# Three of thirty-two zero stores of a decode backward kernel move to GpSimd's queue in pairs of rows, three others to earlier spots on SyncE

## The chip, the cores and the metric

The kernel runs on one core of a Trainium2 chip. The metric is the device time of one execution in microseconds (us). The profile is of one execution of its own; it counts its span from the first instruction of the program to the last.

## What is computed

One decode step of a transformer layer and its gradients, all in bf16, for 4 sequences with one new token each. Cut to what matters:

```python
xn  = layernorm(x)                                     # x: [4, 1, 512]
q   = (xn @ wq)                                        # 32 heads of 128, 8 kv heads
k,v = cache[:, :, Sk - W:, :]                          # Sk = 4096, W = 1024: only the last quarter
out = x + softmax(q k^T / sqrt(128)) v @ wo + (gelu(xn @ w_gate) * (xn @ w_up)) @ w_down
grads = vjp(out)(grad_out)    # of x, k_cache, v_cache, wq, wo, w_gate, w_up, w_down
```

The gradients of the two caches have the caches' whole shape, [4, 8, 4096, 128]. The first 3072 of the 4096 positions take no part in the attention, so their gradients are zero, and the kernel must write those zeros: 2 caches x 4 sequences x 8 heads x 3072 x 128 numbers of two bytes are 50.3 MB. That is 45% of all the bytes that the kernel moves (112.12 MB).

## The kernel before

**Stages.** The feed-forward part comes first (its weights are loaded at the start; its weight gradients are out_6, out_7 and out_8). Then a loop `for t in range(NT)` goes over four groups of two kv heads. Each turn has `pre(t)` (transposed weights, queries and output gradients of the group), `kv_steps(t, 0, ...)` and `kv_steps(t, 1, ...)` (scores with K and with V), the softmax forward and backward, `odq` (the sums over keys), and `fin(t)`. The outer products that make the weight and cache gradients are small pieces in a list `bg`, which `tick(n)` works off between the other steps; each piece evacuates one PSUM bank into a staging tile, and the last piece of a tile stores it.

**The zeros.** `ztile` is a tile of 128 partitions x 6144 zeros. `zlist` holds 32 regions, each two heads of one sequence in out_2 or out_3 (1536 KB). `zero(n)` (L161) takes n regions off the list, or as many as are left, and stores each with one DMA from SyncE (L164) in 128 rows of 12,288 bytes, which all sixteen DMA engines share alike. Calls of `zero` stand at fixed spots of the program: two regions at the start (L168), one after the second `osb_d` store (`zero(f4 == 1)`, L666), one after the first `osb_g` store of each of two weights (L678), one after each store of a cache gradient (L490), two at L721 and in the first turn (L728, L730), `zero(3)` in the last turn (L734), and L755 stores what is left when all else has been issued.

**Queues.** All of SyncE's DMAs go out in program order through one queue. SyncE keeps eight completion semaphores, used in turn, so that a DMA is issued only after the one eight places before it has landed; a store also waits for the engine that fills its tile, and everything behind it waits with it. GpSimd (POOL) issues only the weights of turns 1 to 3, `load_w(t)`, through a queue of its own: `wo_sb` at L123, `wq_sb` at L125. On POOL, `load_w(2)` and `load_w(3)` follow the products `domr` and `qmr` at the end of `pre(1)` and `pre(2)` (L329).

**Buffers.** The pool `stage` holds three staging tiles for the cache gradients (stg_dv, stg_dk), `outp` four for the weight gradients (osb_d, osb_g, osb_o, osb_q). A piece that needs a fresh tile waits until the store of the tile's earlier content has landed. `store` (L100) declares that the stores write disjoint parts of the outputs, so that no store waits for another one for that reason.

Of the kernel before, what the change touches and what calls it, by code (L numbers as in the profile page):

```python
# [18 lines left out]
def kernel(  # L19
# [28 lines left out]
    nc = tc.nc  # L48

    B, Sq, D = A_x.shape  # L50
    _, G, Sk, Dh = A_k_cache.shape
# [4 lines left out]
    K0 = Sk - W  # L56
# [99 lines left out]
    ZR = 2  # L156
    ZW = K0 * Dh * ZR // P
    ztile = const.tile([P, ZW], BF16, name="ztile")
    zlist = deque((og, b, g) for b in range(B) for g in range(0, G, ZR) for og in (out_2, out_3))

    def zero(n=1):  # L161
        for _ in range(min(n, len(zlist))):
            og, b, g = zlist.popleft()
            store(nc.sync, og[b, g:g + ZR, 0:K0, :].rearrange("g (m j) d -> m g (j d)", m=P // ZR), ztile[:], "zeros")  # L164


    nc.gpsimd.memset(ztile[:], 0.0)  # L167
    zero(2)  # L168
    ident_f = const.tile([P, P], FP32, name="ident_f")
    nc.vector.tensor_copy(out=ident_f[:], in_=ident[:])  # L170
    one_f = const.tile([1, 1], FP32, name="one_f")
# [113 lines left out]
    def pre(t):  # L285
        wo_sb, wq_sb = wo_t[t], wq_t[t]
        dq_ps = ps_x.tile([P, 2, HG, B], FP32, name="doq_ps", tag="x")
        held = []

        def do(h2, woT):  # L290
            for i in range(2):
                for c in range(ND):
                    nc.tensor.matmul(dq_ps[:, 0, slot(2 * h2 + i), :], lhsT=woT[:, i, c, :], rhs=dyT[:, c, :],
                                     start=(c == 0), stop=(c == ND - 1))

        for h2 in range(HG // 2):
            ps = transposes([wo_sb[:, 2 * h2 + i, c * P:(c + 1) * P] for i in range(2) for c in range(ND)], "woT")
            woT = tsb.tile([P, 2, ND, P], BF16, name="woT", tag="wT")
            evac(woT[:].rearrange("p i c d -> p (i c d)"), ps[:].rearrange("p x d -> p (x d)"), 1024, half=True)
            held.append((h2, woT))  # L300
            for h in (2 * h2, 2 * h2 + 1):
                for c in range(ND):
                    nc.tensor.matmul(dq_ps[:, 1, slot(h), :], lhsT=wq_sb[:, c, h * Dh:(h + 1) * Dh], rhs=xnT[:, c, :],
                                     start=(c == 0), stop=(c == ND - 1))
            tick(1)
            link()
            if h2:
                do(*held[h2 - 1])
            tick(1)
            link()  # L310
        do(*held[-1])
        T4 = []
        for k, (sc, zt, nm) in enumerate(((None, dom_all[t % 2], "do"), (scale, qm_all[t % 2], "qs"))):
            xT4 = attw.tile([P, B, HG, NQ], BF16, name=nm + "T4", tag=nm + "T4")
            src = dq_ps[:, k].rearrange("p h b -> p b h").unsqueeze(3).broadcast_to([P, B, HG, NQ])
            if sc is None:
                nc.vector.tensor_copy(out=xT4[:], in_=src)
            else:
                nc.scalar.activation(out=xT4[:], in_=src, func=ACT.Copy, scale=sc)
            nc.vector.tensor_copy(out=zt[:, :, SL - 1:].rearrange("p (b g) (r s) -> p b g r s", g=GP, s=SL)[:, :, :, :, 0],  # L320
                                  in_=xT4[:, :, :, 0].rearrange("p b (r g) -> p b g r", g=GP))
            T4.append(xT4)
        tick(2)
        r_ps = transposes([x[:].rearrange("p b h q -> p (b h q)") for x in T4], "r")
        r4 = attw.tile([P, 2, Dh], BF16, name="r4", tag="r4")
        nc.vector.tensor_copy(out=r4[:], in_=r_ps[:])  # L326
        for k, nm in enumerate(("do", "q")):
            mr = attw.tile([P, GP, NQ, Dh], BF16, name=nm + "mr", tag=nm + "mr", bufs=2)
            nc.gpsimd.tensor_tensor(out=mr[:].rearrange("p g q d -> p (g q) d"),  # L329
                                    in0=r4[:, k, :].unsqueeze(1).broadcast_to([P, SL, Dh]),  # L330
                                    in1=msk[:].unsqueeze(2).broadcast_to([P, SL, Dh]),
                                    op=ALU.mult)
            st[t][nm] = mr

    def kv_steps(t, k, links):

# [318 lines left out]
    def piece_d(f4, i, n, held):  # L655
        if i == 0:
            held["osb"] = outp.tile([P, 4, D], BF16, name="osb_d", tag="o")
        m = n * P // 4
        mps = ps_w.tile([P, D], FP32, name="dwd_ps", tag="w")
        nc.tensor.matmul(mps[0:m], lhsT=a_s[:, f4].rearrange("p i f -> p (i f)")[:, i:n * P:4], rhs=dyr[:],  # L660
                         start=True, stop=True)
        evac(held["osb"][0:m, i, :], mps[0:m], 512)
        if i == 3:
            store(nc.sync, out_8[4 * f4 * P:(4 * f4 + n) * P, :].rearrange("(p i) n -> p (i n)", i=4),
                  held["osb"][0:m].rearrange("p i n -> p (i n)"), "rest")
            zero(f4 == 1)  # L666

    def piece_g(s_r, og, c, i, held):
        if i == 0:
# [47 lines left out]
    with tc.tile_pool(name="kv_b", bufs=GP, reuse_waits="tile") as kv_b, \  # L717
            tc.tile_pool(name="w_b", bufs=1, reuse_waits="tile") as w_b, \
            tc.tile_pool(name="stage", bufs=3, reuse_waits="tile") as stage:
        kv_pool[1], w_pool[1] = kv_b, w_b  # L720
        zero()  # L721
        pre(0)
        load_w(1)
        load_kv(1, 0)
        for t in range(NT):
            kv_steps(t, 0, 0)
            if t == 0:
                zero()  # L728
                load_kv(1, 1)
                zero()  # L730
            softmax(t)
            kv_steps(t, 1, 1)
            if t == NT - 1:
                zero(3)  # L734
            link(len(chain))
            softmax_d(t)
            link()
            odq(t, 0)
            load_kv(t + 2, 1)
            if t + 1 < NT:  # L740
                pre(t + 1)
            link(len(chain))
            odT(t, 0)
            odq(t, 1)
            load_kv(t + 2, 0)
            tick(2)
            odT(t, 1)
            fin(t)
            if t + 2 < NT:
                load_w(t + 2)  # L750
            (k0, k1), (o0, o1, q0, q1) = dvdk(t, 1), dw(t)
            for p in (k0, o0, k1, o1, q0, q1):
                bg.extend(p)
        tick(len(bg))
        zero(len(zlist))  # L755

        fin_ps = []
        for o in range(2):
            f_ps = ps_w.tile([B, ND, P], FP32, name="f_ps", tag="w")
            for c in range(ND):  # L760
                nc.tensor.transpose(f_ps[:, c, :], acc[:, o, c, :], ident_f[:])
            fin_ps.append(f_ps)
        acc_o = fin_ps[0][:].rearrange("b c p -> b (c p)")
        acc_d = attw.tile([B, P, ND], FP32, name="acc_d", tag="P_s")
        nc.vector.tensor_copy(out=acc_d[:].rearrange("b p c -> b c p"), in_=fin_ps[1][:])
        acc_d = acc_d[:].rearrange("b p c -> b (p c)")
        out_b = attw.tile([B, D], BF16, name="out_b", tag="pT")
        nc.vector.tensor_tensor(out=out_b[:], in0=acc_o, in1=x4[:], op=ALU.add)
        nc.scalar.dma_start(out=out_0.rearrange("b s d -> (b s) d"), in_=out_b[:])

        s1 = attw.tile([B, 1], FP32, name="s1", tag="m")
        nc.vector.reduce_sum(out=s1[:], in_=acc_d, axis=AX.X)
        pr = attw.tile([B, D], FP32, name="pr", tag="dS_s")
        s2 = attw.tile([B, 1], FP32, name="s2", tag="es")
        nc.vector.tensor_tensor_reduce(out=pr[:], in0=acc_d, in1=xn_f[:], scale=1.0, scalar=0.0,
                                       op0=ALU.mult, op1=ALU.add, accum_out=s2[:])
        nm1 = attw.tile([B, 1], FP32, name="nm1", tag="rr")
        nc.vector.tensor_scalar(out=nm1[:], in0=s1[:], scalar1=-1.0 / D, scalar2=None, op0=ALU.mult)
        nm2 = attw.tile([B, 1], FP32, name="nm2", tag="gs")
        nc.vector.tensor_scalar(out=nm2[:], in0=s2[:], scalar1=-1.0 / D, scalar2=None, op0=ALU.mult)  # L780
        nc.vector.scalar_tensor_tensor(out=pr[:], in0=xn_f[:], scalar=nm2[:, 0:1], in1=acc_d,
                                       op0=ALU.mult, op1=ALU.add)
        nc.vector.tensor_scalar(out=pr[:], in0=pr[:], scalar1=nm1[:, 0:1], scalar2=rstd[:, 0:1],
                                op0=ALU.add, op1=ALU.mult)
        dx_b = attw.tile([B, D], BF16, name="dx_b", tag="E_f")
        nc.vector.tensor_tensor(out=dx_b[:], in0=pr[:], in1=dy4[:], op=ALU.add)
        nc.scalar.dma_start(out=out_1.rearrange("b s d -> (b s) d"), in_=dx_b[:])
# [30 lines left out]
```

## Time and profile before

| what | value |
|---|---|
| median of three runs | 284.95 us (284.80 to 285.53) |
| the profiled execution's own time | 285.34 us |
| its span | 283.4 us |
| busy: PE / DVE / ACT / POOL | 200.5 / 163.4 / 117.8 / 40.1 us |
| moved by DMA | 112.12 MB, mean 396 GB/s |
| SyncE's queue, share of 16 DMA engines' span | 89.5% |
| POOL's queue, the same | 5.6% |
| ACT's queue, the same | 1.8% |
| the 32 zero stores | 1536 KB each, median 19.4 us from issue to landing |

The page of a profile has one part with the span in 40 equal slices of 7.1 us: a digit for each engine (9 is busy for 90% or more), the mean busy share of the sixteen DMA engines, and what they moved. Busy time of the computing engines is an average over the span; here none of them is busy for more than 71% of it, and all of them end well before the span does.

### The profile page before, as it was taken

The page shows a single profiled execution, that of the slowest core. Times are in us where ns is not written, and L with a number is a line of the kernel's source. Part 1 is how long each engine was busy: PE and PEld are TensorE (multiplying, and loading weights), DVE is VectorE, ACT ScalarE, POOL GpSimd, SP SyncE. Part 2 cuts the span into 40 slices and gives each one's busy share as a digit, 9 for nine tenths or more (in the row PEclk, how much of TensorE's full clock was granted, in tenths as well). Part 3 has the DMA queues.
Part 4 walks back from the last instruction along what each step waited for, and adds up shares of the span by engine and source line. Part 5 has one row for each costly group of instructions (what it writes and reads, how often), then busy time and mean ns, then how long its engine had stood idle before and what let it go on. Part 6 is the DMA issues. An engine that isn't in the chain of part 4 may idle for free.

```text
span 283.4 us, 6866 instructions
## 1 busy us (share of the span) xinstructions
PE 200.5 (71%) x2972; PEld 137.3 (48%) x2972; DVE 163.4 (58%) x313; ACT 117.8 (42%) x219; POOL 40.1 (14%) x40
## 2 busy tenths in 40 slices
PE   0275799998798899998993799889995997300000
PEld 0264576765466754676752467665564743100000
DVE  7946646676857455767561576766776288900000
ACT  2021476662156077635371464438661387200000
POOL 8600000043011700020700002130004000000000
PEclk9999579999999999999999599999999799955555
DMA  7999989999999999999999999999999989999993
GB/s 266 391 376 433 432 334 369 370 418 351 366 428 409 419 422 422 426 427 417 410 387 423 423 426 430 410 425 404 397 415 377 415 337 420 426 418 415 422 418 153
DMA packets 19565, 112.12 MB, mean 396 GB/s; under 512 B 1664, under 2 KB 4496, under 8 KB 11088
## 3 DMA queue, kind: packets, MB, share of 16 engines
q1 hardware_dynamic: 17744, 103.56, 89.5%
q0 software_dynamic: 1632, 6.29, 5.6%
q10 hardware_dynamic: 160, 1.84, 1.8%
q8 instruction: 23, 0.38, 0.5%
q14 instruction: 6, 0.05, 0.0%
HBM read 30.68 MB, written 81.01 MB: 394 GB/s over the span
## 4 chain that ended last, share of the span: by engine, by line
PE 30%; issue 19%; DMA 18%; DVE 12%; POOL 5%; ACT 3%; DVEq 0%; POOLq 0%; ACTq 0%
DMA out_dram<-stg_dv 11%; DMA wq_sb<-in_A_wq_dram 7%; PE kv_ps L484 6%; PE T_ps L279 5%; PE od_ps L450 4%; PE S_ps L345 4%; DVE dS_s L367 2%; DVE T_sb L98 2%; PE dwq_ps L520 2%; POOL ztile L167 2%; DVE wqT L98 2%; PE pT_ps L279 2%; PE acc_ps L256 1%; PE dwo_ps L505 1%; DVE P_s L367 1%
## 5 line engine op out<-in xcount | busy, mean ns | idle before, releaser
L98 DVE COPY T_sb<-T_ps 128x1024 bf16<-128x1024 bf16 x64 | 44.1, 688 | 24.9 <-PE T_ps L279 24.7
L97 ACT CAST stg_dk<-kv_ps 128x512 bf16<-128x512 f32 x52 | 29.1, 588 | 26.3 <-PE kv_ps L484 11.5
L97 ACT CAST stg_dv<-kv_ps 128x512 bf16<-128x512 f32 x51 | 28.1, 588 | 25.1 <-PE kv_ps L484 24.4
L484 PE MATMUL kv_ps<-qmr,dS_s 128*128 128x512 bf16 x64 | 23.0, 396 | 7.3 <-ACT stg_dk L97 6.6
L463 POOL TENSOR_TENSOR o_s<-od_r,msk_r 128x512 bf16<-128x512 bf16 x8 | 9.1, 1158 | 107.9 <-DVE od_r L455 78.6
L484 PE MATMUL kv_ps<-domr,P_s 128*128 128x512 bf16 x64 | 21.1, 379 | 0.0
L279 PE MATMUL T_ps<-ident,vb 128*128 128x128 bf16 x256 | 20.3, 225 | 0.3 <-DVE T_sb L98 0.3
L279 PEld LDWEIGHTS <-vb 128*128 128x128 bf16 x256 | 17.2, 101 | 4.9 <-issue 2.7
L279 PE MATMUL T_ps<-ident,kb 128*128 128x128 bf16 x256 | 19.5, 219 | 0.0
L279 PEld LDWEIGHTS <-kb 128*128 128x128 bf16 x256 | 16.7, 98 | 4.2 <-issue 0.9
L97 ACT CAST osb_q<-dwq_ps 128x512 bf16<-128x512 f32 x25 | 14.5, 586 | 8.3 <-PE dwq_ps L520 7.4
L329 POOL TENSOR_TENSOR domr<-r,msk 128x1024 bf16<-128x1024 bf16 x4 | 7.6, 1892 | 68.4 <-DVE r L326 62.0
L97 ACT CAST osb_o<-dwo_ps 128x512 bf16<-128x512 f32 x24 | 13.8, 586 | 4.4 <-PE dwo_ps L505 3.6
L97 ACT CAST osb_g<-dwg_ps 128x512 bf16<-128x512 f32 (+1 forms) x25 | 12.5, 541 | 6.6 <-PE dwg_ps L673 5.0
L98 DVE COPY wgT<-wgT_ps 128x1024 bf16<-128x1024 bf16 x14 | 9.6, 686 | 7.7 <-PE wgT_ps L279 7.7
L345 PE MATMUL S_ps<-T_sb,qm 128*32 128x256 bf16 x128 | 12.7, 386 | 0.6 <-DVE T_sb L98 0.5
L345 PE MATMUL S_ps<-T_sb,dom 128*32 128x256 bf16 x128 | 12.7, 387 | 0.1
L98 DVE COPY woT<-woT_ps 128x1024 bf16<-128x1024 bf16 x16 | 11.0, 686 | 2.6 <-PE woT_ps L279 2.2
L98 DVE CAST stg_dk<-kv_ps 128x512 bf16<-128x512 f32 x12 | 7.9, 686 | 7.8 <-DMA out_dram<-stg_dv 7.2
L505 PE MATMUL dwo_ps<-dyr,o_s 128*128 128x512 bf16 x32 | 11.9, 388 | 0.5 <-DVE stg_dk L98 0.2
L520 PE MATMUL dwq_ps<-od_r,xnm 128*128 128x256 bf16 x64 | 11.6, 274 | 0.2 <-ACT osb_q L97 0.2
L98 DVE COPY wqT<-wqT_ps 128x1024 bf16<-128x1024 bf16 x16 | 10.5, 685 | 1.8 <-PE wqT_ps L279 1.6
(188 smaller groups left out, 377.7 us busy)
## 6 DMA issues: line engine op xcount, KB each, us to landing
out_dram<-ztile SPq DMA_DIRECT2D x32, 1536.0 KB, 19.4
kb<-in_A_k_cache_dram SPq DMA_DIRECT2D x8, 1024.0 KB, 15.7
vb<-in_A_v_cache_dram SPq DMA_DIRECT2D x8, 1024.0 KB, 20.7
out_dram<-stg_dv SPq DMA_DIRECT2D x8, 1024.0 KB, 16.7
out_dram<-stg_dk SPq DMA_DIRECT2D x8, 1024.0 KB, 16.1
out_dram<-osb_o SPq DMA_DIRECT2D x8, 512.0 KB, 19.0
out_dram<-osb_q SPq DMA_DIRECT2D x8, 512.0 KB, 11.6
out_dram<-osb_g SPq DMA_DIRECT2D x8, 448.0 KB, 7.9
```

What stands on the lines that cost most here:

```text
L97: return nc.scalar.copy(out=out, in_=in_)
L98: return nc.vector.tensor_copy(out=out, in_=in_)
L167: nc.gpsimd.memset(ztile[:], 0.0)
L279: nc.tensor.transpose(ps[:, i, :], a, ident[:])
L329: nc.gpsimd.tensor_tensor(out=mr[:].rearrange("p g q d -> p (g q) d"), in0=r4[:, k, :].unsqueeze(1).broadcast_to([P, SL, Dh]), in1=msk[:]. ...
L345: nc.tensor.matmul(ps[b * RB:(b + 1) * RB, :], lhsT=zt[:, b * GP + g, c0:c0 + RB], rhs=T_sb[:].rearrange("p (x b) -> p b x", b=B)[:, b, :] ...
L367: nc.vector.scalar_tensor_tensor(out=out[:], in0=src[:].unsqueeze(2).broadcast_to([P, WQ, B]), scalar=rr[:, 0:1], in1=mskb[:].unsqueeze(1) ...
L450: nc.tensor.matmul(od_ps[g * 32:g * 32 + B * rep, k, g, :], lhsT=cols[:, jj, g * NQ + q, :], rhs=blks[(t, g)][:, j, :], start=(j == 0), st ...
L463: nc.gpsimd.tensor_tensor(out=o_s[:, g], in0=rows[:, g].unsqueeze(1).broadcast_to([P, rep, Dh]), in1=msk_r[:].unsqueeze(2).broadcast_to([P ...
L484: nc.tensor.matmul(mps[:].rearrange("p q d -> p (q d)"), lhsT=src[:, j * P:(j + 1) * P], rhs=mr[:, g].rearrange("p q d -> p (q d)"), start ...
L505: nc.tensor.matmul(mps[:], lhsT=o_s[:, g].rearrange("p r d -> p (r d)")[:, i:rep * Dh:rep], rhs=dyr[:], start=True, stop=True)
L520: nc.tensor.matmul(mps[:, i].rearrange("p g d -> p (g d)"), lhsT=xnm[:, i2 * 2 + i, c * P:(c + 1) * P], rhs=dq_r[:].rearrange("p g d -> p ...
```

## The change

- A new function `zero_pairs()` takes one region off the list and stores it from POOL with eight DMAs of two rows each (one row in each of the region's two heads). Seven of them write 16 x 3456 numbers per row (110,592 bytes); the third (i = 2) writes only the 6144 numbers (12,288 bytes) that are left. The source of DMA i is partition 8i for one row and 8i + 4 for the other; the seven large ones read the same 3456 zeros sixteen times over.
- `zero_pairs()` is called at the end of `pre(t)` for t = 1, 2 and 3. On POOL the eight DMAs stand between `qmr` and `load_w(t + 1)`; those of t = 3 stand before the last two `o_s` products.
- `zero(2)` at the start becomes `zero(3)`; `zero(f4 == 1)` becomes `zero(f4 % 2)`, which also stores one region after the fourth `osb_d` store; `zero(3)` in the last turn becomes `zero(4)`.
- The list of 32 regions is then used up earlier. On SyncE the zero store after the last `stg_dk` and the five at the end are gone; SyncE issues 29 zero stores and POOL the other three regions. Because of the 24 new DMAs on POOL's eight completion semaphores, `load_w(2)` and `load_w(3)` now also wait until the first and second, respectively, of the eight pair stores ahead of them have landed (`wo_sb` for one, `wq_sb` for the other).
- PE, DVE and ACT get the same instructions in the same order.

```diff
+    def zero_pairs():
+
+        if not zlist:
+            return
+        og, b, g = zlist.popleft()
+        zr = og[b, g:g + ZR, 0:K0, :].rearrange("g m d -> g (m d)")
+        w = 27 * Dh
+        r0 = 0
+        for i in range(8):
+            n = 16 * w if i != 2 else K0 * Dh - 7 * 16 * w
+            if i != 2:
+                src = ztile[8 * i:8 * i + 8, 0:w].rearrange("(a x) w -> a x w", a=2)[:, 0, :].unsqueeze(1).broadcast_to([2, 16, w])
+                dst = zr[:, r0:r0 + n].rearrange("g (r w) -> g r w", r=16)
+            else:
+                src = ztile[8 * i:8 * i + 8, 0:n].rearrange("(a x) w -> a x w", a=2)[:, 0, :]
+                dst = zr[:, r0:r0 + n]
+            store(nc.gpsimd, dst, src, "zeros")
+            r0 += n
+
...
     nc.gpsimd.memset(ztile[:], 0.0)
-    zero(2)
+    zero(3)
...
             st[t][nm] = mr
+        if t:
+            zero_pairs()
...
                   held["osb"][0:m].rearrange("p i n -> p (i n)"), "rest")
-            zero(f4 == 1)
+            zero(f4 % 2)
...
             if t == NT - 1:
-                zero(3)
+                zero(4)
```

## The prediction

> **What bounds the kernel now.** I read the page's 40 slices first, then SyncE's DMA issues in order of time, the waits of SyncE, the chain that ended last, and POOL's timeline.
>
> The slices (digits, then GB/s) and the totals:
>
> ```profile
> span 283.4 us, 6866 instructions
> DMA  7999989999999999999999999999999989999993
> GB/s 266 391 376 433 432 334 369 370 418 351 366 428 409 419 422 422 426 427 417 410 387 423 423 426 430 410 425 404 397 415 377 415 337 420 426 418 415 422 418 153
> HBM read 30.68 MB, written 81.01 MB: 394 GB/s over the span
> ```
>
> The DMA engines are the bound: they are busy in nearly every slice, at 415 to 430 GB/s, and slow down in a few places only. The end is pure DMA. Columns of the next two fences: start, length, what, count.
>
> ```profile
> 18.55 1.69 SPq L103 DMA_DIRECT2D out_dram<-ztile  x2
> 37.73 3.53 SPq L103 DMA_DIRECT2D out_dram<-osb_d  x2
> 43.08 3.79 SPq L103 DMA_DIRECT2D out_dram<-osb_d  x2
> 49.16 0.33 SPq L103 DMA_DIRECT2D out_dram<-osb_g  x1
> 211.52 3.15 SPq L103 DMA_DIRECT2D out_dram<-osb_q  x2
> 214.72 3.80 SPq L103 DMA_DIRECT2D out_dram<-ztile  x3
> 228.66 0.54 SPq L103 DMA_DIRECT2D out_dram<-stg_dv  x1
> 253.96 6.89 SPq L103 DMA_DIRECT2D out_dram<-ztile  x5
> ```
>
> The five last zero stores (7.9 MB) are issued when everything else is done. SyncE has nothing to issue around 41, 48 and 228 us, and the queue runs dry there. The waits of SyncE and the chain:
>
> ```profile
> SPq L813 <- DMA out_dram<-ztile: 21.2, 5, 6.7
> ...
> 65.59 18.90 DMA wq_sb<-in_A_wq_dram
> ...
> 132.89 23.57 DMA out_dram<-stg_dv
> ...
> 228.66 7.99 DMA out_dram<-stg_dv
> ...
> 247.74 0.68 DVE dx_b L786
> ```
>
> At the end SyncE waits 21.2 us for five zero stores. Compute ends at 248.4 us, 35 us before the span, so it has slack, and three of its own stalls are on DMAs. POOL:
>
> ```profile
> 94.35 1.89 POOL L329 TENSOR_TENSOR qmr<-r,msk 128x1024 bf16<-128x1024 bf16 x1
> 96.18 0.93 POOL L123 DMA_DIRECT2D wo_sb<-in_A_wo_dram  x1
> 97.73 0.76 POOL L125 DMA_DIRECT2D wq_sb<-in_A_wq_dram  x1 [0.61 <-PE wqT_ps L279]
> ```
>
> Two more readings come from the trace's DMA records. First, each DMA has sixteen completions, one for each engine. Those of the very last store come at 279.0 to 279.2 (fourteen), 279.9 and 282.3 us, so one engine, call it A, sets the end and another, B, is second. A is behind all along: 6.7 us at 156, 6.9 at 190, 5.1 at 221. Followed back from its last packet, A shows no gap of more than 0.06 us down to 71 us: it never idles, so filling the dry spots gives A nothing after 71 us. A's sequence also has no room for the four-row stores of out_0 and out_1, which use four engines. Second, in 2 us bins the mean idle time of an engine is about 1.2 us at 40 to 42, 1.05 at 48 to 52 (together 2.25), and after 196 us 2.5 in five spots, 1.2 of it at 228.
>
> [...]while GpSimd's weights (4,096-byte packets) run beside SyncE's larger ones, at 100 to 116 us, they get 118 to 147 of about 423 GB/s.[...]
>
> **The change part by part.** The bytes stay the same; what can change is idle time, the balance of the engines, and compute's slack.
>
> *Balance.* One region gives each engine 1536 KB / 16 = 98,304 bytes. As pairs it gives fourteen engines 110,592 and two 12,288. Three regions take 258 KB from the two; at 26.2 bytes/ns (a 12,288-byte packet of the before trace takes 0.469 us on average) that is 9.85 us less. The other fourteen get 36.9 KB more, 1.45 us at 25.5 bytes/ns (between the 4,096- and 8,192-byte packets' 24.6 and 25.7). If the two are A and B, A would end at 282.3 - 9.85 = 272.5 and no longer decides. The third engine, D, then does (279.2 us).
>
> *Early fills.* The third store at the start covers the dry spot at 41, the one after the fourth osb_d that at 48 to 51. D idles there about as the mean does, so up to 2.25 us go; I take 2.0. Cost: every osb_d and osb_g store behind them lands up to 3.6 to 7.4 us later (1536 KB at 425 GB/s is 3.7 us), and outp has four tiles, so the feed-forward part may stall for 0 to 3 us. That is compute time, covered by its slack.
>
> *Late fills.* The 2.5 us after 196 belong to the fast engines. D, like A, was behind at each of these spots (2 us at 225) and hardly idled; the fills bring D about 0.2 us at most. I count nothing; at best, if D's lag is shaken up by the new order, 2 us.
>
> [...]I take 0.5 in all, since the weights that ran beside the stores showed no loss of total throughput (423 GB/s).
>
> *POOL's issue and the weights behind it.* Eight issues of 0.76 to 1.06 us each (the wo_sb and wq_sb rows) are 6 to 8.5 us; load_w(2) moves from 96.2 to about 104. It also waits for the first two pair stores, and on each ring its packets stand behind theirs. 110,592 bytes per engine at 40% of 26 bytes/ns are 10.6 us, so the pairs run from 97 to between 108 and 114; wo_sb and wq_sb (128 KB per engine at the 126 GB/s of before) take 16.6 us more: 124 to 130. In before wq_sb landed at 119.7 and was needed at about 126. So pre(2) stalls 0 to 4 us; load_w(3) before landed at 162 and is needed at 174, so it stalls 0 to 1. The pairs of t = 3 have only two o_s products behind them, needed late. Of these DMAs' waits nothing reaches the end of the span unless compute loses its slack.
>
> *Compute's slack.* The last matrix product of the pieces ends at 242.4, dx_b lands at 253.9: 11.5 us later. Before it stand six more regions than in before, 22 us if each delayed it fully; 242.4 + 22.2 + 11.5 = 276, still just under the DMA end below. zero(4) in the last turn lengthens the stg waits at 228 by up to 3.7 us; this is in the 22.
>
> *The last five stores.* They vanish from the end (18.3 us of transfers), but their bytes delay what went before, so as such this gains nothing.
>
> Sum: 279.2 - 2.0 + 1.45 + 0.5 = 279.15 us for D, then 1.1 us from last completion to the span's end (282.3 to 283.4): span 280.2, or 3.2 us less. The profiled execution took 285.34, of which 1.96 lie outside the span, and is 0.39 above the median; against the median: 284.95 - 3.2 = 281.75. Some of the late fill should reach D, because its lag comes and goes; with 0.75 of the 2 us I say 281.0.
>
> **Rivals.**
> - *A is not 4 or 5.* For it: nothing in the profile names A; one engine only is far behind, and it might be any of the twelve that out_0 leaves. Against: the two engines that are behind at the end fit a pair. A then gets 1.45 us more and regains what it idled before 71 us, at most 1: about 285.4, no difference.
> - *Late weights (slower than before).* Place: POOL and its ring at pre(2) and pre(3). If the pair stores get 20% instead of 40% of an engine they last 21 us; wo_sb and wq_sb land some 11 us later still, and the stalls are about 14 and 8 us. With 7 from the early stores and 4 from zero(4), 242.4 + 33 = 275, plus 11.5 is 287, plus 1.1 and 2: about 289. It decides once compute's last product comes after 270, that is from 28 us of delay on. For it: 65.59 18.90 above shows how slow that queue is beside a full one. Against: A's smaller lag frees the stage tiles earlier (in the 23.57 us wait A was the last by 6.7), which gives compute time back.
> - *The pairs don't walk.* If all eight used the same two engines, these would get 786 KB each per region instead of 98, 27 us more, 81 for three: about 360. Slower by far. For it: the profile shows no store of two rows on POOL's queue.[...]
> - *Everything balances.* If all idle time is filled for every engine, 279.0 - 4.75 + 1.45 = 275.7, 6.6 us below 282.3: 278.3.
>
> **How the numbers follow.** Forecast 281.0 (279 to 283.5): 0.48. Full balance 278.3: 0.14. A elsewhere, 285.4: 0.15. Late weights, 289: 0.16. No walk, 360: 0.07. This measurement can tell about 0.3%, 0.85 us, from no change: faster means under 284.1, slower over 285.8. Faster: the first two and some of the third, 0.65; same 0.11, from the third; slower 0.24. The range from 277.0 to 287.5 leaves out the fifth case and the worse part of the fourth; the likeliest case's own range is 279 to 283.5.
>
> **What would show it.** Right: the last store's completions lie within about 2 us, none 3 us behind; no dry spot at 41 and 48; POOL's queue carries 11 MB instead of 6.3; SyncE's last wait is no longer 21 us; dx_b lands before the last store. Wrong: one engine still 3 us behind (A elsewhere); PE waiting over 8 us for wo_sb or wq_sb in pre(2) (late weights); two completions far after all others (no walk). What would make the forecast wrong most easily is D: its 279.2 comes from one profiled execution.

## The result, and the profile after

| kernel | median (range) | runs |
|---|---|---|
| before | 285.12 us (284.80 to 285.53) | 4 |
| after | 323.92 us (321.13 to 326.36) | 4 |

The ratio is 1.133, with a 95% interval from 1.125 to 1.140: the change costs 38.8 us. The forecast was 281.0 us. The profiled execution took 326.36 us, the longest of the four, and the ratio leaves it out (as it does for the run with nine long rows below). Its span is 324.6 us, 41.2 us more than that of before.

The page of the changed kernel, its slices, its DMA totals, its queues (q1 is SyncE's, q0 POOL's, q10 ACT's: packets, MB, share of the 16 engines' span) and the row of the pair stores among its DMA issues (8.1 us per slice here):

```profile
span 324.6 us, 6889 instructions
...
DMA  7999999999999999998209999982099999999992
GB/s 292 373 406 427 429 419 426 421 396 384 425 420 423 422 398 400 374 352 349 116 2 358 380 401 382 362 283 106 0 359 281 320 385 407 422 420 420 425 368 86
DMA packets 24942, 112.15 MB, mean 345 GB/s; under 512 B 6746, under 2 KB 9578, under 8 KB 16842
...
q1 hardware_dynamic: 17312, 98.84, 76.5%
q0 software_dynamic: 7440, 11.03, 10.3%
q10 hardware_dynamic: 160, 1.84, 1.6%
...
out_dram<-ztile POOLq DMA_DIRECT2D x21, 216.0 KB, 31.0
```

Three things are to be seen. The dry spots at 41 and 48 us of before are gone (slices 6 to 8 now carry 419, 426 and 421 GB/s). In their place the DMA engines stand idle twice, in slices 20 and 21 and in 28 and 29 (down to 2 and 0 GB/s); by the DMA records an engine idles on average 15.2 us between 130 and 175 us and 15.7 between 200 and 250. And while the bytes are the same to 0.03 MB, there are 5,377 more packets, 5,082 of them under 512 bytes, although no row of the new stores is shorter than 6,912.

Idle time isn't all of the loss. The shares of the three queues come to 88.4% of 324.6 us here and to 96.9% of 283.4 us before, 287 and 275 us of packet time per engine. So some 29 of the 41.2 us are more idle time of the engines, and 12 are more time in packets.

Why the engines stand idle is in the waits (engine and line, what it waited for: us in total, times, longest) and in the chain that ended last (start, length):

```profile
ACT stg_dv L97 <- PE kv_ps L505: 79.4, 20, 32.6
...
PEld L298 <- DMA wo_sb<-in_A_wo_dram: 44.4, 2, 24.4
PE woT_ps L298 <- DMA wo_sb<-in_A_wo_dram: 44.1, 2, 24.3
...
POOL wo_sb L123 <- PE kv_ps L505: 22.8, 2, 12.4
...
PEld L322 <- DMA wq_sb<-in_A_wq_dram: 6.9, 2, 5.1
```

```profile
122.55 37.39 DMA wq_sb<-in_A_wq_dram
...
198.28 27.54 DMA wq_sb<-in_A_wq_dram
...
281.27 18.72 DMA out_dram<-stg_dv
```

TensorE waits for `wo_sb` of turns 2 and 3, 24.4 and 20.0 us, and then for `wq_sb`, 6.9 us in all. In the kernel before there was no wait for `wo_sb`, and 0.7 us for `wq_sb`. The 44.4 us are about the 41.2 that the span grew by. POOL's timeline (start, length, what, and in brackets the idle time before) shows where the load got late:

```profile
99.05 1.89 POOL L348 TENSOR_TENSOR qmr<-r,msk 128x1024 bf16<-128x1024 bf16 x1
100.88 4.69 POOL L103 DMA_DIRECT2D out_dram<-ztile  x8
115.94 0.92 POOL L123 DMA_DIRECT2D wo_sb<-in_A_wo_dram  x1 [10.36 <-PE kv_ps L505]
122.55 0.78 POOL L125 DMA_DIRECT2D wq_sb<-in_A_wq_dram  x1 [5.68 <-PE dwq_ps L541]
```

The two brackets name TensorE, but it isn't TensorE that POOL waits for: the first pair store lands at 115.36 us and the second at 121.98, each some 0.6 us before the issue. This is the wait for a free completion semaphore: `wo_sb` uses that of the first pair store, `wq_sb` that of the second (by the trace the completions of POOL's 30 DMAs stand on eight semaphores, 64 on each of six and 48 on each of two). By the trace's completion records the last of the eight pair stores lands at 148.3 us, `wo_sb` at 154.1 (before: 111.1) and `wq_sb` at 159.9 (119.7). Both are issued long before 148.3, yet the first of their 4,096-byte packets starts only at 136.7, 20.8 us after the issue of `wo_sb`. So it is the pair stores ahead of them on the rings, and not the late issue, that decides when they land. SyncE's timeline closes the circle:

```profile
132.02 5.08 SPq L133 DMA_DIRECT2D vb<-in_A_v_cache_dram  x2
169.37 0.60 SPq L103 DMA_DIRECT2D out_dram<-stg_dv  x1
```

For 32 us SyncE issues nothing, because the next store in its order needs a `stg_dv` tile that TensorE has not filled. So compute waits for a load, and then the DMA engines wait for compute.

### The profile page after: what moved, and what is told of

The parts are those of the page before. It is cut to its first block, busy times and chain, and to the rows that moved or that the text cites. A ratio compares the mean times of both kernels' runs of the same rounds, so it can differ in the third digit from the quotient of the medians.

```text
span 324.6 us, 6889 instructions
## 1 busy us (share of the span) xinstructions
PE 207.7 (64%) x2972; PEld 141.5 (44%) x2972; DVE 164.1 (51%) x313; ACT 118.3 (36%) x219; POOL 54.3 (17%) x64
## 4 chain that ended last, share of the span: by engine, by line
PE 41%; DMA 37%; DVE 12%; ACT 4%; issue 2%; SPq 0%; DVEq 0%; ACTq 0%
DMA wq_sb<-in_A_wq_dram 20%; PE kv_ps L505 8%; PE T_ps L298 8%; DMA out_dram<-stg_dv 6%; DMA wd_sb<-in_B_w_down_dram 5%; PE S_ps L366 5%; PE od_ps L471 4%; DMA out_dram<-osb_g 4%; DMA out_dram<-osb_d 3%; PE acc_ps L275 2%; DVE T_sb L98 2%; PE dwo_ps L526 2%; DVE wqT L98 2%; PE woT_ps L298 2%; PE pT_ps L298 2%
## 5 line engine op out<-in xcount | busy, mean ns | idle before, releaser
L298 PE MATMUL woT_ps<-ident,wo_sb 128*128 128x128 bf16 x128 | 12.7, 258 | 44.2 <-DMA wo_sb<-in_A_wo_dram 44.1
L97 ACT CAST stg_dk<-kv_ps 128x512 bf16<-128x512 f32 x52 | 29.3, 589 | 30.6 <-DMA out_dram<-stg_dv 11.6
L298 PEld LDWEIGHTS <-wo_sb 128*128 128x128 bf16 x128 | 10.8, 121 | 45.9 <-DMA wo_sb<-in_A_wo_dram 44.4
L505 PE MATMUL kv_ps<-domr,P_s 128*128 128x512 bf16 x64 | 24.0, 426 | 0.0
L298 PE MATMUL T_ps<-ident,kb 128*128 128x128 bf16 x256 | 20.6, 226 | 0.0
L298 PE MATMUL T_ps<-ident,vb 128*128 128x128 bf16 x256 | 19.4, 219 | 0.3 <-DVE T_sb L98 0.3
L298 PEld LDWEIGHTS <-kb 128*128 128x128 bf16 x256 | 17.6, 102 | 4.5 <-issue 1.5
L298 PEld LDWEIGHTS <-vb 128*128 128x128 bf16 x256 | 16.4, 98 | 4.6 <-issue 2.4
L505 PEld LDWEIGHTS <-dS_s 128*128 128x128 bf16 x64 | 6.0, 98 | 19.4 <-issue 18.2
L103 POOL DMA_DIRECT2D out_dram<-ztile x24 | 14.1, 594 | 0.0
L98 DVE CAST stg_dv<-kv_ps 128x512 bf16<-128x512 f32 x13 | 8.7, 684 | 8.9 <-PE kv_ps L505 8.9
```

What stands on the lines that cost most here:

```text
L97: return nc.scalar.copy(out=out, in_=in_)
L98: return nc.vector.tensor_copy(out=out, in_=in_)
L103: d = eng.dma_start(out=out, in_=in_)
L298: nc.tensor.transpose(ps[:, i, :], a, ident[:])
L505: nc.tensor.matmul(mps[:].rearrange("p q d -> p (q d)"), lhsT=src[:, j * P:(j + 1) * P], rhs=mr[:, g].rearrange("p q d -> p (q d)"), start ...
```

## What the packets are

The trace's DMA records give each packet with its queue, size, start and length, but not its engine. A count or a time per engine is below a sixteenth of the sum over all engines, and the sixteen completions of a DMA are read as one for each engine. "Ring" stands below for one engine's part of a queue.

In the kernel after, POOL's queue carries 672 packets of 6,912 bytes and 6 of 12,288, the zeros; 1,536 of 4,096, the weights; and 5,226 of 4 bytes. Before has 96 of those, as many as its six weight loads have completions (sixteen each). After has 480 completions of POOL's 30 DMAs, so 4,746 packets of 4 bytes are left over; they are called fillers below. Their number is exactly 21 x 14 x 16 + 3 x 14 x 1 = 4,746: it comes out if a store of two rows has its data on two engines and puts as many fillers on each of the fourteen others as a data engine gets packets. That is a reading of the count, since no record names an engine. The starts and lengths agree as to the two: of the first twenty 6,912-byte packets never more than two run at once, and the first fourteen, 262 ns each, start in two rows of seven, each 0.72 us after the one before it in its row. By this account every engine has 7 x 17 + 2 = 121 packets of each region on POOL's ring. A whole region in 128 rows has 9 (the run with such regions has 2,064 packets on POOL's queue, 432 more than before, which are 3 x 16 x 9).

The next table counts, for the first region after `pre(1)` in each kernel, the packets per engine on POOL's ring and on SyncE's between the first packet of the region and the middle completion of its last store:

```
stores of the region              by form   POOL : SyncE    lasted    us per packet
after, 16 x 6,912 B per row         121    122.1 : 123.0    40.4 us      0.33
nine rows of 12,288 B                72     72.4 : 73.9     29.4         0.41
16 x 2,080 B                         65     65.1 : 66.4     24.2         0.37
16 x 1,024 B                         37     36.6 : 36.9     14.0         0.38
one store of 128 rows                 9     10.1 : 11.4      7.9         0.78
before: wo_sb and wq_sb alone         -     33.4 : 35.2     16.9         0.51
```

In every row the two counts are close to each other, from 10.1 and 11.4 up to 122.1 and 123.0: the two rings took turns, one packet each, whatever the sizes. The sums agree in short stretches too: the second to fourth 2 us of the first region in after have 80 packets of POOL's and 81 of SyncE's, 90 and 90, 88 and 86. In the 40.4 us of the first line an engine spends on average only 5.9 us on POOL's packets; the rest is the packets of SyncE's ring that go between. A four-byte filler is done in about 9 ns but cost a whole turn, about one packet of SyncE's by the 122.1 to 123.0. (In the second and third region of after the counts are less even, 116.3 to 103.0 and 111.8 to 70.9. The third starts when SyncE has next to nothing on its rings: 550 packets of POOL's and 46 of SyncE's in the first 2 us.)

The theory to be tested: **the pair stores cost as many turns as they have packets, and the weights behind them wait that long.** Its rivals: the three zero stores that SyncE issues earlier cost the time; the bytes on POOL's queue do; or the position ahead of the weights does.

## The experiments

Each edit is to the kernel after, unless the text names another run; cuts in an edit are marked by three dots. Ratios are to the kernel before on the same chip, with 95% intervals.

**No pair stores.** SyncE's three moves alone; the three regions stay in the list and are stored at the end.

```diff
-        if t:
-            zero_pairs()
```

> The pair stores are left out, the three other zero stores stay at their earlier spots, and three regions are again stored at the end from SyncE. Theory T (the pair stores' many packets on POOL's ring hold up the weights behind them): about 282 us, between 279 and 285.5, no wait for wo_sb above 5 us. Rival E (the zeros issued earlier on SyncE push loads back): stays above 305.

Measured: 283.36 us, ratio 0.991 (0.987 to 0.994), faster than both kernels. The page:

```profile
span 281.6 us, 6857 instructions
...
DMA  7999999999999999999999999999999999999990
GB/s 272 385 375 432 427 435 413 421 412 425 361 389 424 388 409 425 425 418 422 420 406 408 423 425 425 424 407 413 381 379 414 406 413 423 425 417 420 412 404 24
```

No slice between the first and the last is dry, and nothing waits for the weights: `wo_sb` and `wq_sb` land at 114.6 and 123.1. The last store's completions come at 274.6 to 275.0 (thirteen engines), 275.7, 275.8 and 280.5: one engine, A if it is the same as before, is 5.5 us behind the thirteen and alone sets the end. Without the pair stores there is no loss; the moves on SyncE gain 0.9%.

**The pair stores alone.** The three moves on SyncE undone.

```diff
-    zero(3)
+    zero(2)
...
-            zero(f4 % 2)
+            zero(f4 == 1)
...
-                zero(4)
+                zero(3)
```

> Only the pair stores, without the three earlier zero stores on SyncE. Theory T: the waits for wo_sb stay above 15 us each, 312 to 328. Rival E (the loss needs SyncE's queue to be fuller by the earlier zeros): under 300.

Measured: 327.58 us, 1.145 (1.141 to 1.149). The wait is the same as in after, a little longer:

```profile
PEld L298 <- DMA wo_sb<-in_A_wo_dram: 46.5, 2, 25.8
```

So the moves on SyncE bring 2 to 4 us also beside the pairs: the two kernels are 41.2 and 38.8 us above before, each against its own chip, and 327.58 and 323.92 us as such.

**The same bytes on the same queue in 9 packets.** In place of `zero_pairs()` a whole region in 128 rows, from POOL, at the same spot.

```diff
-            zero_pairs()
+            zero(1, nc.gpsimd)
```

> The three regions stay on POOL's queue at the same place ahead of the weights, but each as one store of 128 rows of 12,288 bytes: 9 packets on each engine's ring instead of 121, the same bytes. Theory T (count of packets): about 282, between 279 and 287, no long wait for wo_sb. Rival B (bytes ahead of the weights on the ring): 98 KB per engine still stand ahead, so wo_sb still lands over 10 us late and the time stays above 300.

Measured: 284.14 us, 0.994 (0.992 to 0.996). The page, with the bytes of after on POOL's queue (q0), its packets fewer and no slice dry:

```profile
DMA  7999999999999999999999999999999999999960
...
q0 software_dynamic: 2064, 11.01, 9.7%
```

`wo_sb` and `wq_sb` land at 121.5 and 129.7, 7 us later than without a store ahead of them, and nothing waits for them. The bytes and the place ahead of the weights together cost some 0.8 us (284.14 against 283.36 on the same chip); the form of the stores costs the rest.

**Whole regions in more packets.** Two stores per region with two pieces of 3,072 bytes per partition, meant to make many more packets.

```diff
+            for h in range(ZR):
+                store(eng, og[b, g + h, 0:K0, :].rearrange("(m x j) d -> m x (j d)", m=P, x=2),
+                      ztile[:, 0:ZW // 4].unsqueeze(1).broadcast_to([P, 2, ZW // 4]), "zeros")
...
-            zero_pairs()
+            zero(1, nc.gpsimd)
```

> The three regions on POOL ahead of the weights as two full-width stores each, in pieces of 3,072 bytes: 34 packets on each engine's ring per region instead of 9, the same bytes, no store on two engines. Theory T: against the run with whole regions, wo_sb of pre(2) lands 7 to 10 us later (128 to 132 us) and the time is 284 to 291. Rival S (the skew between engines alone, not the count, holds up the weights): wo_sb lands at 121 to 124 and the time stays within 1 us of 284.1.

Measured: 284.03 us, 0.993 (0.990 to 0.995). The pieces were put together in pairs to 6,144 bytes, so that there are 18 packets per engine and region and not 34, and `wo_sb` met neither recorded range. Twice the packets of the run above bring `wo_sb` in at 125.0 and `wq_sb` at 133.1, 3.5 us later; 9 turns of some 0.38 us are 3.4. Here every store has 128 rows, so it is the count alone that moves the weights.

**Fewer or lighter packets at the same spot.** Three variants of the two-row stores. The first has nine rows of 12,288 bytes in place of sixteen, all bytes written. The others write only the first 1,024 or 2,080 bytes of each of the sixteen pieces, which leaves 84% or 69% of the three regions unwritten.

```diff
-                ... .broadcast_to([2, 16, w])
-                dst = zr[:, r0:r0 + n].rearrange("g (r w) -> g r w", r=16)
+                ... .broadcast_to([2, 9, ZW])                                        # nine long rows
+                dst = zr[:, r0:r0 + n].rearrange("g (r w) -> g r w", r=9)
...
+                ... .broadcast_to([2, 16, 512])                                      # 1,024 bytes
+                dst = zr[:, r0:r0 + n].rearrange("g (r w) -> g r w", r=16)[:, :, 0:512]
...
+                ... .broadcast_to([2, 16, 1040])                                     # 2,080 bytes
+                dst = zr[:, r0:r0 + n].rearrange("g (r w) -> g r w", r=16)[:, :, 0:1040]
```

> The pair stores carry the same bytes on the same engines, but in 9 rows of 12,288 bytes instead of 16 of 6,912: 7 x 10 + 2 = 72 packets on each engine's ring per region instead of 121. Theory T (a packet of POOL's ring waits for one packet of SyncE's, whatever its size): a region takes about 27 us instead of 43, the waits for wo_sb fall by about 15 us each, 285 to 305 us in all. Rival B (bytes that two engines carry at a time): unchanged, 318 to 328.

> The large pair stores write only the first 512 of each 3456 numbers (1,024 bytes), so 85% of the three regions is not written: the same number of packets (121 per engine and region), a sixth of the bytes (about 3.9 MB less, some 9 us of all engines). Theory T (count of packets): PE still waits over 15 us each for wo_sb in pre(2) and pre(3), the time is 300 to 320. Rival B (bytes on the ring[...]): the waits vanish and the time is under 285.

> The large pair stores write only the first 1,040 of each 3456 numbers, so 69% of the three regions is not written; [...]each engine should still carry 121 packets per region with 30% of the bytes (some 7.5 us less for all engines). Theory T: each region still takes 36 to 43 us and PE waits over 12 us each for wo_sb in pre(2) and pre(3); 300 to 316 us. Rival B (bytes): as with the short rows before, under 285.

Measured: nine long rows 318.75 us, 1.110 (1.104 to 1.116); 1,024 bytes 277.87 us, 0.972; 2,080 bytes 295.17 us, 1.033 (1.027 to 1.039). The waits for `wo_sb`, first with nine long rows, then with 2,080 bytes; with 1,024 bytes there is none. (With those for `wq_sb` they are 46.7, 29.3 and 14.1 us, against 51.3 in after.)

```profile
PEld L298 <- DMA wo_sb<-in_A_wo_dram: 38.3, 2, 20.1
```

```profile
PEld L298 <- DMA wo_sb<-in_A_wo_dram: 19.3, 2, 10.5
```

None of the three times lies where the theory had put it. Nine long rows and 1,024 bytes came out in the ranges of the rival B, bytes, and 2,080 bytes in neither.

Two expectations rested on a wrong premise: the short pieces were not one packet each. By the records four pieces of 1,024 bytes share a packet of 4,096, and two of 2,080 share one of 4,160, so a region had 37 and 65 packets, not 121. The fillers follow, one for each data packet: the records have 1,176 of 16 bytes (21 x 14 x 4) and 2,352 of 8 bytes (21 x 14 x 8). By the table the time of a region goes with the packets: 121, 72, 65 and 37 of them took 40.4, 29.4, 24.2 and 14.0 us. The nine long rows carry all the bytes and 60% of the packets, and took 73% of the time; the 2,080-byte run has 31% of the bytes and 54% of the packets, and took 60%. Against the full pairs, nine rows change the packets alone, and the region gets 11.0 us shorter; so the count matters. Against the 2,080 bytes, nine rows have three times the bytes and nearly the same count, and last 5.2 us longer; so the bytes matter too. And the time in all hardly follows: nine rows were to take 15 us off each wait and took 6.1 off the two together, which the theory doesn't explain. A turn lasted 0.41 us there, and the second mechanism below stays. The two light runs also move 4.0 and 3.2 MB less, some 9 and 8 us at 420 GB/s, so their times are not to be set against the full kernels'.

**The pair stores behind the weights.** Now no load stands behind them.

```diff
-        if t:
-            zero_pairs()
...
                 load_w(t + 2)
+            if t + 1 < NT:
+                zero_pairs()
```

> The same pair stores, called after load_w(t + 2) instead of before it, so that no weight stands behind them on POOL. Theory T: the waits of PE for wo_sb fall from 44 us to under 5 and the time to 279 to 290. Rival P (stores of two rows slow the DMA engines as such[...]): the pairs still run, so the time stays above 300 and SyncE's queue moves under 400 GB/s beside them.

Measured: 308.80 us, 1.080 (1.075 to 1.085). The theory's expectation missed: TensorE's wait for `wo_sb` is gone, yet the time stays 23 us above before on the same chip. It is the rival P that named a time above 300, and SyncE's queue under 400 GB/s; from 105 to 161 us, beside the pairs, it moves 314. The waits and the chain show another place (for comparison, the waits of before first):

```profile
ACT stg_dk L97 <- DMA out_dram<-stg_dv: 7.6, 2, 6.7
DVE stg_dk L98 <- DMA out_dram<-stg_dv: 7.2, 2, 6.2
```

```profile
ACT stg_dk L97 <- DMA out_dram<-stg_dv: 48.0, 3, 23.7
DVE stg_dk L98 <- DMA out_dram<-stg_dv: 47.0, 3, 23.9
```

```profile
141.44 26.28 DMA out_dram<-stg_dv
...
193.00 28.27 DMA out_dram<-stg_dv
...
253.90 28.67 DMA out_dram<-stg_dv
```

The evacuations wait for a staging tile, whose store lands late. A store lands with the last of its completions: that of `stg_dv` issued at 193.00 us has its sixteen between 197.3 and 221.3, 24.0 us apart, and the chain has it landed 28.27 us after its issue; the corresponding one of before has 6.6 (186.8 to 193.4). The explanation that suggests itself is skew, an estimate from the counts above: if a pair store puts 110,592 bytes on each of two engines, 4.2 us at the 26.4 bytes/ns of a 6,912-byte packet in 262 ns, and nothing but fillers on the others, the two fall behind on SyncE's ring, then the two of the next store.

**Behind the weights, in whole regions or light.** Two runs to test the skew, both edits to the run before: whole regions in place of the pairs, and the pairs with 2,080 bytes per piece (69% of the three regions unwritten, edited as above).

```diff
             if t + 1 < NT:
-                zero_pairs()
+                zero(1, nc.gpsimd)
```

> The three regions on POOL as whole stores of 128 rows, called after load_w(t + 2) instead of before it. Theory T: no store of few engines, few packets: 281 to 285, weights of pre(2) land as in the run with SyncE's moves only (wq_sb at 123, not 130). Rival P (any zero store on POOL's ring costs, in whatever place): above 287.

> The pair stores after the weights, with only 1,040 of each 3456 numbers (69% of the three regions is not written; some 7.5 us less of DMA time for all engines). In the run with full pairs after the weights the stores of stg_dv landed late (48 us of waits on ACT and DVE). Theory K (skew: the data of a pair store hold up SyncE's packets on two engines at a time, so each of SyncE's DMAs lands with the engine that is behind): a third of the bytes, so the waits for stg_dv fall under 25 us and the time is 276 to 286. Rival C (the count of packets on POOL's ring also slows SyncE's queue): the waits stay above 35 us and the time above 295.

Measured: whole regions 284.10 us, 0.993 (0.990 to 0.997), and light pairs 278.94 us, 0.974 (0.970 to 0.978), with these waits for `stg_dv`, whole regions first:

```profile
ACT stg_dk L97 <- DMA out_dram<-stg_dv: 24.2, 3, 15.2
```

```profile
ACT stg_dk L97 <- DMA out_dram<-stg_dv: 18.9, 2, 10.7
DVE stg_dk L98 <- DMA out_dram<-stg_dv: 18.5, 2, 10.8
```

The spot behind the weights harms nothing as such, nor do waits of 24 us: the whole regions ahead of the weights had 24.8, and much the same time. The light pairs keep the two-row form and the fillers, with 65 packets per region, and the store of `stg_dv` that corresponds has its completions 8.8 us apart (193.1 to 201.9), not 24.0; with whole regions they are 10.7 apart. The 3.2 MB that they don't write explain at most 8 of the 30 us between the two times. This supports the skew, which would need much data on few engines. It isn't a proof. Packets (54%) and bytes (31%) were cut together; that the extra wait vanished altogether (18.9 us, under the 24.2 of whole regions), and didn't shrink by half with the packets, speaks for the data. And the rival P stands in part: in the run with full pairs the three queues' packet time is 287 us per engine (93.4% of 307.3), 12 more than in before, so packets beside the pairs also take longer. The runs don't part this from the skew.

**Which engine is A?** In the kernel without pair stores the last region is stored by SyncE as two stores of six or twelve rows. By the trace's completion records such a store has six or twelve completions, so it is read as running on six or twelve engines; which engines they are the trace doesn't tell. The engine numbers in the prediction and in the expectations, 4 and 5 for the two of the small pair store and the others, are assumptions of the author that no run shows. First the rows came from neighbouring partitions.

```diff
-        zero(len(zlist))
+        zero(len(zlist) - 1)
+        og, b, g = zlist.popleft()
+        for h in range(ZR):
+            store(nc.sync, og[b, g + h, 0:K0, :].rearrange("(e x j) d -> e x (j d)", e=6, x=16),
+                  ztile[0:6, 0:4096].unsqueeze(1).broadcast_to([6, 16, 4096]), "zeros")
```

> As the run with SyncE's moves only, but the last region goes as two stores whose slowest dimension is 6[...]; these get 164 KB more, the other ten 98 KB less (3.75 us). In that run one engine, A, ended 5.5 us after the rest. If A is 4 or 5 (as the forecast took it): A alone ends last at about 287, five others at about 281, time about 289. If A is one of 6 to 15: six engines end together at about 281 and A before them at about 277; time about 284.

> The same with a slowest dimension of 12[...]. If A is one of 12 to 15, it ends at about 277 beside the twelve at 276, and the time falls to about 279.5. If A is one of 4 to 11, it ends at about 282, and the time is about 284.5.

Measured: 315.23 us, 1.100 (1.096 to 1.105), and 294.22 us, 1.028 (1.024 to 1.032), outside both ranges each time, and far longer than the engines' share of bytes. With six rows, four of the six completions of the second store came at 312.1 to 312.7 us and two at 288.8 and 292.0; with twelve, all came between 286.9 and 291.2. The bytes per engine don't explain this, so both were repeated with the source rows 20 and 10 partitions apart (edit to the run with six rows):

```diff
-                  ztile[0:6, 0:4096].unsqueeze(1).broadcast_to([6, 16, 4096]), "zeros")
+                  ztile[0:120, 0:4096].rearrange("(a x) w -> a x w", a=6)[:, 0, :].unsqueeze(1).broadcast_to([6, 16, 4096]), "zeros")
```

> e1 (no pair stores) with the last region stored by SyncE as two stores of six rows, from partitions 0, 20, 40, 60, 80 and 100[...]. Each of the six engines gets 262 KB per store, 524 KB in all, 426 KB more than a sixteenth of the region, which is 16 us at 26 bytes/ns. In e1 the last completions are 275 us (thirteen to fifteen engines) and 280.5 (A). If A is one of the first six engines (A is 4 or 5, as the prediction took it): one of the six completes some 5 us after the five others (five near 287, one near 292). If A is another engine: the six complete within 2 us of each other near 287, A ends near 277, and the time is about 289 instead of 294.

> The same with two stores of twelve rows, from partitions 0, 10, 20 to 110. Each of the twelve engines gets 131 KB per store, 262 KB in all, 164 KB more than a sixteenth, which is 6.3 us less what e1's last region took from them already: twelve near 277, four near 271. If A is among the first twelve: one of the twelve completes some 5 us later, near 283, and the time is about 285. If A is one of the last four: the twelve lie within 2 us, A ends at about 277 too, and the time is about 279 to 280, faster than e1's 283.4.

Measured, one run each: 289.47 and 286.24 us (before on the same chip: 285.16). With six rows the last completions are 280.9, 281.0, 281.1, 281.2, 282.0 and 286.5 us. The expectation had counted the bytes of a store twice (131 KB per engine, not 262), hence five near 281 and not 287, and its time of 289 for "A is another engine" is met by that mistake alone. That one of the six is some 5 us behind the other five is what it named for "A among the first six". The late engine also goes step by step with them: it ends at 276.7 in the full-width store before, at 281.6 in the first and 286.5 in the second six-row store, 4.9 us each, as the others do. So A, if it is the engine that is behind here too, is one of the six that the six-row stores use. That it is one of the two that the small pair stores are for was not shown. The prediction's reading that A takes no part in the stores of out_0 and out_1, four rows and by the trace four completions each, doesn't show it either: it rests on a sequence pieced together from starts and ends, since the records name no engine, and in most places more than one packet fits. The run with twelve agrees, with one engine last at 283.2, but says less: of the other eleven, six ended at 275.8 to 276.7 and five at 280.0 to 281.2, which no run here explains.

## Why the prediction was wrong

- **The step that failed** is *POOL's issue and the weights behind it*: "110,592 bytes per engine at 40% of 26 bytes/ns are 10.6 us, so the pairs run from 97 to between 108 and 114". They ran from 101 to 148. A share of bandwidth was taken from before, where POOL's packets had 4,096 bytes, and applied to a queue whose turns are mostly four-byte fillers. The region's 1.57 MB in 40.4 us are 39 GB/s, about a tenth of what all queues move and not 40%. In turns the sum is 121 packets per engine at 0.33 us, 40 us, and `wo_sb` and `wq_sb` come behind them: 154.1 and 159.9 us, not "124 to 130". The stalls for `wo_sb` are 24.4 and 20.0 us, not "0 to 4" and "0 to 1". That the eight issues take 4.69 us, not 6 to 8.5, doesn't matter beside this.
- *The rival Late weights* named the place, the wait and the point of decision (the last product comes after 270), but its size (289 us: pairs of 21 us, stalls of 14 and 8) came from the same kind of share, halved; its own terms add up to 290. The packets of the pair stores could have been counted from the access patterns, except for the fillers, which nothing before the change showed.
- *Compute's slack* of 22 us was used up: the last product of the pieces (`f_ps` follows it) ends at 306.95 us instead of 242.39, and the span ends 17.7 us later, after the last store. Without the pairs it ends at 253.16: 10.8 us are the price of the three earlier zeros, the other 53.8 that of the pairs, 51.3 of them the waits for `wo_sb` and `wq_sb`.
- *Early fills* was right in kind. Without the pairs the dry spots are gone, and thirteen engines end at 274.6 to 275.0 instead of 279.0 to 279.2. These 4.3 us are more than the 2.0 counted; *Late fills*, counted at nothing, probably hold part of it, but which spot gives what wasn't tried. The last engine gains 1.8 us (282.3 to 280.5), a little more than the 1 that the rival with A elsewhere allowed, and it sets the time of that kernel.
- *Balance*: the division of a region among fourteen engines with 110,592 bytes and two with 12,288 was an assumption, and no record names an engine. That A is among the engines of the six-row stores is supported by that run, that it is 4 or 5 by none. "Behind all along" says too much: the 6.7 us at 156 are the distance to the first engine, and the last completion (156.5) is 0.7 us after the one before it. Only later does one engine stand apart, by some 2 us at 197 and 3.6 at 226. What the pairs would gain by sparing it can't be seen: in after the sixteen last completions lie between 312.8 and 323.3 us, and no engine stands out.
- The 0.5 us that the prediction took for a loss of throughput beside the pairs wasn't isolated. Packets did take longer beside them: 12 us more per engine in all, some 2.7 of them the fillers; a 12,288-byte packet of SyncE's took 486 ns on average instead of 469, and a 6,912-byte packet of the pairs 341, though over half of them took 262. The reason stays open. *The pairs don't walk* doesn't fit: in the third region up to eleven 6,912-byte packets run at once, while the first twenty of the first region never ran more than two at once. Which engines the stores used isn't shown.
- What no step had is that full-width stores land late beside the pairs, their completions up to 24.0 us apart. With the pairs behind the weights this costs 23 us, so the layout can't be saved by a better place alone. Skew is the likely reason, not a shown one.

The best kernel with all zeros written is that without pair stores, 283.36 us; whole regions on POOL (284.03 to 284.14) are no better. To spare A in another way wasn't tried.

## What to carry to other kernels

Before a DMA goes ahead of a load on the same queue, count the packets that it puts on each engine's ring and multiply by the packet time of the busy ring beside it. Here, with the 0.33 us per turn that were measured afterwards, that gives 40 us where a share of bandwidth had given 10.6. It is a first estimate only: with nine long rows the waits fell by less than the count. A transfer of two rows was not free for the packets beside it here (123.0 packets of SyncE's per engine went while it had 122.1), and full-width stores beside it landed late, with completions 24.0 us apart instead of 6.6, so that buffers came free late. An idle DMA engine late in a kernel can be the last link of a chain: find the load that compute waits for, then the queue behind which it was issued.

## What the runs showed of the hardware that had not been expected

- On GpSimd's queue 24 stores of two rows came with 4,746 packets of four bytes beyond their completions, as many as if each store put one on each of fourteen engines for every packet of a data engine. Where the pieces were put together, so were these: 2,352 of 8 bytes with two pieces to a packet, 1,176 of 16 bytes with four.
- While both had work, two rings alternated packet by packet, 122.1 to 123.0 as the mean of the engines, with sizes from 4 to 12,288 bytes; a packet of zeros and a filler counted as one turn each.
- GpSimd's queue put short pieces together: four of 1,024 bytes to packets of 4,096, two of 2,080 to 4,160 or of 3,072 to 6,144; pieces of 6,912 and 12,288 bytes stayed alone (672 and 6 packets in after).
- Six-row stores from neighbouring partitions were slower than from partitions 20 apart, 315.23 against 289.47 us; only the source partitions differ between the two runs. With the rows from partitions 0 to 5, four engines moved 524 KB in the 20.5 us between the ends of two stores (291.6 to 312.1), 25.6 bytes/ns together; with the rows 20 partitions apart, each engine moved its 131 KB in 4.9 us (276.0 to 280.9), 26.7 bytes/ns. What holds the four to this was not shown.
